# The assignment check of a mixture-of-experts kernel as an all-engine `If`, with list, weights and transposes in another order

## The chip, the cores and the metric

The program runs on one core of one Trainium2 chip. The metric is the device time of one execution, in microseconds. A core has TensorE (PE; its weight loads are shown apart as PEld), VectorE (DVE), ScalarE (ACT), GpSimd (POOL) and SyncE (SP), each with its own instruction queue, and 16 DMA engines that all queues share.

## What is computed

Two parts, one behind the other. A linear attention runs over 4 batches, 8 heads, 768 steps and head width 48. Its output, as 3072 rows ("tokens") of 384 numbers, goes through a balanced mixture of 8 experts: each expert takes exactly 3072 / 8 = 384 tokens. The assignment is greedy over all logits in falling order, and each expert is a two-layer network with 1024 hidden numbers, in float32:

```python
    logits = x @ w_gate
    order = np.argsort(-logits.flatten())
    for idx in order:
        tok, e = (int(idx) // E, int(idx) % E)
        if assigned[tok] >= 0 or counts[e] >= cap:
            continue
        assigned[tok] = e
        counts[e] += 1
    for e in range(E):
        mask = assigned == e
        h = np.maximum(x[mask] @ w1[e], 0.0)
        out[mask] = h @ w2[e]
```

## The kernel before

The program has three stretches. The first, some 205 us, is the attention. It is written twice, `attention_mild` for decays near one and `attention_any` for others, and an `If` on all engines (L975) chooses; with these inputs the mild arm runs. It works through 24 units of 128 tokens, writes their rows to memory (`x_rows`) and their logits to the tile `LG`. The second stretch finds the first expert's tokens. The third, from about 243 us to the end, is the loop over the experts.

**The assignment.** Instead of sorting, `Assignment` fills one expert at a time. A token proposes to the expert of its highest logit; the expert whose 384th proposal has the highest logit is filled first. `likely` (L726) finds that bound by three rounds of `count` (L671). Each round compares every token's maximum `m` with 16 candidates on VectorE (`ind`), sums over tokens on TensorE (`each`, three matmuls of 128 columns of weights), picks and folds on VectorE (`own`, `cnt`, `wide`), spreads the sums on TensorE (`all_ps`), and picks the next candidates on VectorE. The results are `fmax` (which expert), `acc` (which tokens) and `place` (the token's place in the expert's list). If the count of accepted tokens is exactly 384 and the expert is the only one, `flag` (L791) is 1. Otherwise `surely` (L797) does the whole thing exactly, in eight rounds of counts. With these inputs the flag is 1 each time, so `surely` never runs, but its code stands in the program.

`fill` (L695) runs `likely`, loads the flag into a register of TensorE and of VectorE (L703), and chooses between the two bodies of a `Switch` on these two engines (L705): `surely`, or nothing. Then `leave` (L713 to L724) strikes out the expert's column and the accepted tokens in `LG` and brings `taken` and `last` up to date. `remainder` (L869) does the last expert, without a check.

**The list.** `tokens` (L902) turns `place` into `tok`, the numbers of the 384 tokens, as three columns of 128: five VectorE operations up to `vals`, six matmuls (L919), two VectorE operations, one matmul (L929), and two VectorE operations up to `tok` (L936).

**The expert loop.** `fetch` for the expert that comes next does, in this order: `load_weights` (a number on VectorE, a register load on SyncE at L996, and two DMAs of 1.5 MB each on SyncE's queue, L999 and L1001), `tokens`, three indirect DMAs on GpSimd's queue that gather 128 rows of 384 numbers each (L1010), and the transposes: for each of the three blocks of 128 tokens three matmuls against the identity (L1016) and one copy by ScalarE (L1017). `expert` does the network: eight blocks of the hidden layer (`h_ps`, L1025), with a Relu on ScalarE for each (L1026), then three blocks of outputs (`o_ps`, L1030), each copied by ScalarE (L1032) and scattered by an indirect DMA of GpSimd (L1033). A float32 matmul of 128x128x384 is two instructions in the trace, so the hidden layer is 48 and an output block 16.

**What sets the order.** The code of turn n is: `fill` and `fetch` for expert n+1, then `expert` for n. A planner turns it into the queues of the engines: it goes by the order of the code, and where an instruction's inputs are not there yet by its estimate, it puts later ones ahead of it. So hidden matmuls of expert n stand between the counts for expert n+1. The body of a conditional stays together as one piece. Each engine then runs its own queue strictly in that order.

**PSUM.** There are eight banks. Before, the assignment uses three (`each`, `all_ps`, and one that its other results share), the transposes one, the hidden and the output blocks two each. Weights, gathered rows (`xg`) and their transposes (`xT`) have two buffers each, `tok` has three.

Of the kernel before, what the change touches and what calls it, by code (L numbers as in the profile page):

```python
# [10 lines left out]
F32 = mybir.dt.float32  # L11
# [7 lines left out]
PSUM = bass.MemoryType.PSUM  # L19
# [493 lines left out]
class Assignment:  # L513
# [17 lines left out]
    ND = 16  # L531
    G = 8
# [135 lines left out]
    def tt(self, out, a, b, op):  # L668
        self.nc.vector.tensor_tensor(out=out, in0=a, in1=b, op=op)  # L669

    def count(self, pool, m, prop, cand, digit_of):  # L671

        nc, ps, tt = self.nc, self.ps, self.tt
        NT, E, ND, G = self.NT, self.E, self.ND, self.G
        ind = pool.tile([128, NT, ND], BF16, name="ind")
        tt(ind, self.by_token(m, ND), self.by_expert(cand), ALU.is_ge)
        each = ps.tile([128, G, E], F32, name="each")
        for j in range(NT // G):
            nc.tensor.matmul(each.rearrange("p i e -> p (i e)"),  # L679
                             ind[:, ts(j, G), :].rearrange("p i d -> p (i d)"),  # L680
                             prop[:, ts(j, G), :].rearrange("p i e -> p (i e)"),
                             start=(j == 0), stop=(j == NT // G - 1))
        own = pool.tile([128, G, E], F32, name="own")
        tt(own, each, self.same, ALU.mult)
        cnt = pool.tile([128, E], F32, name="cnt")
        nc.vector.tensor_reduce(out=cnt, in_=own.rearrange("p i e -> p e i"), axis=AX.X, op=ALU.add)
        wide = pool.tile([128, ND, E], F16, name="wide")
        tt(wide, digit_of.unsqueeze(2).to_broadcast([128, ND, E]),
           cnt.unsqueeze(1).to_broadcast([128, ND, E]), ALU.mult)
        all_ps = ps.tile([128, ND, E], F32, name="all_ps")  # L690
        nc.tensor.matmul(all_ps.rearrange("p d e -> p (d e)"), self.ones_h,
                         wide.rearrange("p d e -> p (d e)"), start=True, stop=True)
        return all_ps

    def fill(self):  # L695

        nc = self.nc
        out = dict(fmax=self.outs.tile([128, 1], F32, name="fmax"),
                   acc=self.outs.tile([128, self.NT], BF16, name="acc"),
                   place=self.outs.tile([128, self.NT], I32, name="place"))  # L700
        flag = self.likely(**out)
        engines = (mybir.EngineType.PE, mybir.EngineType.DVE)
        sure = nc.values_load(flag[0:1, 0:1], engines=engines, min_val=0, max_val=1,  # L703
                              skip_runtime_bounds_check_because="a truth value")
        for arm in self.tc.Switch({e: sure for e in engines}, 2):  # L705
            if arm == 0:
                with ExitStack() as part:
                    pool = part.enter_context(self.tc.tile_pool(name="surely", bufs=1))
                    self.surely(pool, **out)
        self.leave(out["fmax"], out["acc"])  # L710
        return out["fmax"], out["place"]

    def leave(self, fmax, acc):  # L713

# [154 lines left out]
    def remainder(self):  # L869

        nc, pool = self.nc, self.pool
        sel = pool.tile([128, 2, self.NT], BF16, name="sel")
        nc.vector.memset(sel[:, 1, :], 0.0)
        nc.vector.tensor_scalar(out=sel[:, 0, :], in0=self.taken, scalar1=-1.0, scalar2=1.0,
                                op0=ALU.mult, op1=ALU.add)
        fmax = self.outs.tile([128, 1], F32, name="fmax")
        nc.vector.tensor_scalar(out=fmax, in0=self.last, scalar1=-1.0, scalar2=float(self.E),
                                op0=ALU.mult, op1=ALU.add)
        acc = self.outs.tile([128, self.NT], BF16, name="acc")
        place = self.outs.tile([128, self.NT], I32, name="place")  # L880
        self.places(pool, sel, acc, place)
        return fmax, place

    def places(self, pool, sel, acc, place):

# [55 lines left out]
def rwkv5_eagle_then_base_layer_balanced(  # L941
# [12 lines left out]
    nc = tc.nc  # L954
    N, DX = out.shape
    E, _, F = moe_w1.shape
    NT = N // 128
    CAP = N // E
    NC = CAP // 128
    KD = DX // 128  # L960
    KF = F // 128
# [8 lines left out]
    walk = Assignment(ctx, tc, LG, CAP)  # L970
# [12 lines left out]
    out_rows = dram_disjoint_views(out, NT)  # L983
    wpool = ctx.enter_context(tc.tile_pool(name="weights", bufs=2))
    xpool = ctx.enter_context(tc.tile_pool(name="f_x", bufs=2))
    hpool = ctx.enter_context(tc.tile_pool(name="f_h", bufs=2))
    opool = ctx.enter_context(tc.tile_pool(name="f_o", bufs=3))
    ps_t = ctx.enter_context(tc.tile_pool(name="f_ps_t", bufs=1, space=PSUM))
    ps_h = ctx.enter_context(tc.tile_pool(name="f_ps_h", bufs=2, space=PSUM))
    ps_o = ctx.enter_context(tc.tile_pool(name="f_ps_o", bufs=2, space=PSUM))  # L990

    def load_weights(fmax):
        number = xpool.tile([1, 1], I32, name="number")
        nc.vector.tensor_scalar(out=number, in0=fmax[0:1, :], scalar1=-1.0, scalar2=float(E),
                                op0=ALU.mult, op1=ALU.add)
        e = nc.values_load(number[0:1, 0:1], engines=(mybir.EngineType.SP,), min_val=0, max_val=E - 1,  # L996
                           skip_runtime_bounds_check_because="E less a number from 1 to E")
        w1 = wpool.tile([128, KD, F], F32, name="w1")
        nc.sync.dma_start(w1, moe_w1[ds(e, 1)].rearrange("o (c p) f -> p (o c) f", p=128))  # L999
        w2 = wpool.tile([128, KF, DX], F32, name="w2")  # L1000
        nc.sync.dma_start(w2, moe_w2[ds(e, 1)].rearrange("o (c p) d -> p (o c) d", p=128))  # L1001
        return w1, w2

    def fetch(fmax, place):
        w1, w2 = load_weights(fmax)
        tok = walk.tokens(place)
        xg = xpool.tile([128, NC, DX], F32, name="xg")
        xT = xpool.tile([128, KD, CAP], F32, name="xT")
        for c in range(NC):
            nc.gpsimd.indirect_dma_start(  # L1010
                out=xg[:, c, :], out_offset=None, in_=x_dram,
                in_offset=bass.IndirectOffsetOnAxis(ap=tok[:, c:c + 1], axis=0))
        for c in range(NC):
            xT_ps = ps_t.tile([128, KD, 128], F32, name="xT_ps")
            for f in range(KD):
                nc.tensor.transpose(xT_ps[:, f, :], xg[:, c, ts(f, 128)], ident)  # L1016
            nc.scalar.copy(xT[:, :, ts(c, 128)], xT_ps)  # L1017
        return w1, w2, tok, xT

    def expert(n, w1, w2, tok, xT):  # L1020
        hid = hpool.tile([128, KF, CAP], F32, name="hid")
        for j in range(KF):
            h_ps = ps_h.tile([128, CAP], F32, name="h_ps")
            for f in range(KD):
                nc.tensor.matmul(h_ps, w1[:, f, ts(j, 128)], xT[:, f, :], start=(f == 0), stop=(f == KD - 1))  # L1025
            nc.scalar.activation(hid[:, j, :], h_ps, AF.Relu)  # L1026
        for c in range(NC):
            o_ps = ps_o.tile([128, DX], F32, name="o_ps")
            for j in range(KF):
                nc.tensor.matmul(o_ps, hid[:, j, ts(c, 128)], w2[:, j, :], start=(j == 0), stop=(j == KF - 1))  # L1030
            o_sb = opool.tile([128, DX], F32, name="o_sb")
            nc.scalar.copy(o_sb, o_ps)  # L1032
            nc.gpsimd.indirect_dma_start(  # L1033
                out=out_rows[n * NC + c], out_offset=bass.IndirectOffsetOnAxis(ap=tok[:, c:c + 1], axis=0),
                in_=o_sb, in_offset=None)

    ahead = fetch(*walk.fill())
    for n in range(E):
        here = ahead
        if n + 1 < E:  # L1040
            ahead = fetch(*(walk.fill() if n + 2 < E else walk.remainder()))
        expert(n, *here)


# [26 lines left out]
```

## Time and profile before

| | us |
|---|---|
| median of 3 runs | 593.01 |
| the three runs | 591.62, 593.01, 596.58 |
| the profiled execution | 591.62 |
| its span, first to last instruction | 589.9 |
| busy: PE, DVE, POOL, ACT | 460.3, 217.4, 139.5, 124.3 |
| last attention work of TensorE | 205.5 |
| first hidden matmul | 243.38 |

The mean granted TensorE clock is 0.917 of full speed. The page shows one execution; times in its views count from the first instruction, in microseconds unless marked ns. A row of the timeline names the start, the length, the engine, the source line, the operation with `out<-in` and shapes, and in brackets the idle time of the engine before it with what ended that. A row of a line's view gives least, median and most length in nanoseconds. A "q" behind an engine's name (PEldq) means its sequencer: loads of registers, branches and semaphore waits, which are not counted as busy. Line 1066 is the end of the program, where the pieces of a `Switch` are put in.

The page's slices of the GB/s row show the weights of each expert as a burst (232 to 289 GB/s in the slice in which they come), with little traffic between the bursts.

### The profile page before, as it was taken

To read this page: it belongs to the slowest core of one execution; us is meant where nothing else is said; L and a number is where in the kernel's file an instruction comes from. 1 tells how busy PE (TensorE), PEld (TensorE's weight loads), DVE (VectorE), ACT (ScalarE), POOL (GpSimd) and SP (SyncE) were. 2 spreads that over 40 slices of the span, in tenths; PEclk is the share of its full clock that TensorE was granted. 3 is DMA by queue.
4 is the path that set the end of the run, shared out by engine and by line. 5 is a ranking of instruction groups with operands and counts; after the bars stand their busy time and mean duration, and the time that the engine had idled before them with its cause. 6 is when DMAs were issued, how large, how long until landed. Compare 5 with 4: busy or idle time off the path is not lost. (4 is left out here: it accounts for less than half of the span.)

```text
span 589.9 us, 6607 instructions
## 1 busy us (share of the span) xinstructions
PE 460.3 (78%) x2310; PEld 322.7 (55%) x2310; DVE 217.4 (37%) x664; ACT 124.3 (21%) x255; POOL 139.5 (24%) x178
## 2 busy tenths in 40 slices
PE   0489999999999810569958958959958965999995
PEld 0379888888899700335534524525524533655553
DVE  4787665555572264330251251142142142020000
ACT  0335333333334100112111111111111110121110
POOL 5655555445521002010102101201201201120101
PEclk9999999999999755679979988998998998899999
DMA  6456544444321005260116116107107008250001
GB/s 131 96 110 144 111 102 105 104 98 99 74 54 56 29 4 190 69 232 24 41 24 236 40 14 246 40 4 254 40 5 254 35 10 289 101 160 14 27 1 40
DMA packets 93957, 54.71 MB, mean 93 GB/s; under 512 B 77105, under 2 KB 88498, under 8 KB 93874
## 3 DMA queue, kind: packets, MB, share of 16 engines
q1 hardware_dynamic: 86402, 39.33, 24.3%
q0 software_dynamic: 3072, 9.44, 4.8%
q10 hardware_dynamic: 4400, 4.93, 2.8%
q8 instruction: 40, 0.66, 0.5%
q14 instruction: 43, 0.35, 0.2%
HBM read 44.25 MB, written 9.44 MB: 91 GB/s over the span
## 5 line engine op out<-in xcount | busy, mean ns | idle before, releaser
L1025 PE MATMUL h_ps<-xT,w 128*128 128x384 f32 x384 | 147.7, 534 | 40.3 <-issue 40.3
L1030 PE MATMUL o_ps<-w,hid 128*128 128x384 f32 x384 | 130.3, 493 | 0.0
L1025 PEld LDWEIGHTS h_ps<-xT,w 128*128 128x128 f32 x384 | 74.2, 207 | 88.7 <-issue 58.7
L1030 PEld LDWEIGHTS o_ps<-w,hid 128*128 128x128 f32 x384 | 72.9, 193 | 47.3 <-issue 0.6
L1010 POOL DMA_INDIRECT xg<-x_rows,tok x24 | 23.5, 978 | 204.4 <-PE h_ps L1025 97.2
L1026 ACT ACTIVATE hid<-h_ps 128x384 f32<-128x384 f32 x64 | 31.4, 491 | 152.7 <-PE h_ps L1025 149.3
L1033 POOL DMA_INDIRECT out_dram<-o_sb,tok x24 | 23.6, 985 | 149.4 <-ACT o_sb L1032 124.4
L454 PE MATMUL y_ps<-vt,AT 128*128 128x48 f32 x384 | 46.8, 275 | 2.5 <-DVE AT L437 2.5
L669 DVE TENSOR_TENSOR own<-each,same 128x64 f32<-128x64 f32 x21 | 4.7, 224 | 118.0 <-PE each L679 118.0
L454 PEld LDWEIGHTS y_ps<-vt,AT 128*128 128x128 f32 x384 | 46.1, 195 | 2.9 <-DVE AT L437 2.7
L432 PE MATMUL g_ps<-rB,kT 96*128 96x256 f32 x192 | 45.9, 379 | 0.0
L437 DVE TENSOR_TENSOR AT<-g_ps,mask 128x512 f32<-128x512 f32 x48 | 30.9, 685 | 25.3 <-PE g_ps L432 25.2
L432 PEld LDWEIGHTS g_ps<-rB,kT 96*128 96x128 f32 x192 | 34.6, 191 | 3.6
L397 POOL TENSOR_TENSOR rk<-rt,kt 128x384 f32<-128x384 f32 x24 | 23.9, 998 | 34.9 <-issue 22.5
L1032 ACT COPY o_sb<-o_ps 128x384 f32<-128x384 f32 x24 | 11.5, 479 | 94.7 <-PE o_ps L1030 71.2
L420 ACT ACTIVATE rB<-rT_ps,own 96x512 f32<-96x512 f32 x48 | 30.5, 680 | 3.3 <-PE rT_ps L415 2.6
L1016 PE MATMUL xT_ps<-ident,xg 128*128 128x128 f32 x72 | 14.8, 322 | 20.8 <-DMA xg<-x_rows,tok 15.9
L402 POOL TENSOR_TENSOR yd<-vt,dd 128x384 f32<-128x384 f32 x24 | 20.8, 868 | 36.6 <-DVE xt L458 36.0
L482 ACT COPY xT<-xT_ps 128x384 f32<-128x384 f32 x24 | 11.5, 479 | 80.3 <-PE xT_ps L480 80.3
L1017 ACT COPY xT<-xT_ps 128x384 f32<-128x384 f32 x24 | 11.5, 479 | 76.3 <-PE xT_ps L1016 43.1
L1016 PEld LDWEIGHTS xT_ps<-ident,xg 128*128 128x128 f32 x72 | 8.9, 158 | 33.5 <-DMA xg<-x_rows,tok 20.3
L392 DVE TENSOR_TENSOR ks<-kt,wk 128x384 f32<-128x384 f32 x24 | 24.9, 1048 | 2.6 <-PE kv_ps L465 2.6
(166 smaller groups left out, 490.7 us busy)
## 6 DMA issues: line engine op xcount, KB each, us to landing
w<-in_moe_w_dram SPq DMA_DIRECT2D x16, 1536.0 KB, 7.9
kt<-in_k_dram SPq DMA_DIRECT2D x24, 192.0 KB, 3.1
rt<-in_r_dram SPq DMA_DIRECT2D x24, 192.0 KB, 3.0
vt<-in_v_dram SPq DMA_DIRECT2D x24, 192.0 KB, 2.9
x_rows<-xt ACTq DMA_DIRECT2D x24, 192.0 KB, 2.0
xg<-x_rows,tok POOLq DMA_INDIRECT x24, 3.5
out_dram<-o_sb,tok POOLq DMA_INDIRECT x24, 2.6
u_bc<-in_u_dram ACTq DMA_DIRECT2D x1, 192.0 KB, 4.4
```

The costliest lines, as they stand in the source:

```text
L392: nc.vector.tensor_mul(ks, kt, wk)
L397: nc.gpsimd.tensor_mul(rk, rt, kt)
L420: nc.scalar.activation(rB[:, :, q, :], rT_ps, AF.Copy, scale=own[:, q:q + 1])
L432: nc.tensor.matmul(g_ps[:, 2 * a:2 * a + 2, :].rearrange("p q t -> p (q t)"), kT[:, a, :], rB[:, a].rearrange("p q t -> p (q t)"), start=T ...
L437: nc.vector.tensor_mul(AT[:, hs, :], g_ps[:, hs, :], mask.unsqueeze(1).to_broadcast([128, HP, T]))
L454: nc.tensor.matmul(y_ps[:, ds(h * D, D)], AT[:, h, :], vt[:, ds(h * D, D)], start=first, stop=(h == H - 1), skip_group_check=True)
L1010: nc.gpsimd.indirect_dma_start(out=xg[:, c, :], out_offset=None, in_=x_dram, in_offset=bass.IndirectOffsetOnAxis(ap=tok[:, c:c + 1], axis=0))
L1016: nc.tensor.transpose(xT_ps[:, f, :], xg[:, c, ts(f, 128)], ident)
L1025: nc.tensor.matmul(h_ps, w1[:, f, ts(j, 128)], xT[:, f, :], start=(f == 0), stop=(f == KD - 1))
L1026: nc.scalar.activation(hid[:, j, :], h_ps, AF.Relu)
L1030: nc.tensor.matmul(o_ps, hid[:, j, ts(c, 128)], w2[:, j, :], start=(j == 0), stop=(j == KF - 1))
L1033: nc.gpsimd.indirect_dma_start(out=out_rows[n * NC + c], out_offset=bass.IndirectOffsetOnAxis(ap=tok[:, c:c + 1], axis=0), in_=o_sb, in_of ...
```

## The change

It has five parts.

1. `fill` loads the flag on all engines, and an `If(found < 1)` on all engines takes the place of the `Switch` on two. With the flag at 1 the body, `surely`, is jumped.
2. `tokens` is called in `fill`, ahead of `leave`; the list is made before the expert is struck out.
3. `fetch` issues the gather first and asks for the weights behind it.
4. The transposes leave `fetch`. They become `turn`, called ahead of the last of the three output blocks of the expert at hand; for the first expert ahead of the loop. The network is split into `hidden` and `result` for that.
5. The two results of `count` share one bank (`counts`; columns 0 to 63 and 128 to 255), and the bank that this frees goes to the transposes, which then have two.

The core of the diff:

```diff
@@ count
-        each = ps.tile([128, G, E], F32, name="each")
+        bank = ps.tile([128, 512], F32, name="counts")
+        each = bank[:, 0:G * E].rearrange("p (i e) -> p i e", e=E)
+        all_ps = bank[:, 128:128 + ND * E].rearrange("p (d e) -> p d e", e=E)
...
-        all_ps = ps.tile([128, ND, E], F32, name="all_ps")
@@ fill
-        engines = (mybir.EngineType.PE, mybir.EngineType.DVE)
-        sure = nc.values_load(flag[0:1, 0:1], engines=engines, min_val=0, max_val=1,
-                              skip_runtime_bounds_check_because="a truth value")
-        for arm in self.tc.Switch({e: sure for e in engines}, 2):
-            if arm == 0:
-                with ExitStack() as part:
-                    pool = part.enter_context(self.tc.tile_pool(name="surely", bufs=1))
-                    self.surely(pool, **out)
+        found = nc.values_load(flag[0:1, 0:1], min_val=0, max_val=1,
+                               skip_runtime_bounds_check_because="a truth value")
+        with self.tc.If(found < 1):
+            with ExitStack() as part:
+                pool = part.enter_context(self.tc.tile_pool(name="surely", bufs=1))
+                self.surely(pool, **out)
+        tok = self.tokens(out["place"])
         self.leave(out["fmax"], out["acc"])
-        return out["fmax"], out["place"]
+        return out["fmax"], tok
@@ remainder
-        return fmax, place
+        return fmax, self.tokens(place)
@@ the experts
-    ps_t = ctx.enter_context(tc.tile_pool(name="f_ps_t", bufs=1, space=PSUM))
+    ps_t = ctx.enter_context(tc.tile_pool(name="f_ps_t", bufs=2, space=PSUM))
...
-    def fetch(fmax, place):
-        w1, w2 = load_weights(fmax)
-        tok = walk.tokens(place)
+    def fetch(fmax, tok):
         xg = xpool.tile([128, NC, DX], F32, name="xg")
-        xT = xpool.tile([128, KD, CAP], F32, name="xT")
         for c in range(NC):
             nc.gpsimd.indirect_dma_start(
                 out=xg[:, c, :], out_offset=None, in_=x_dram,
                 in_offset=bass.IndirectOffsetOnAxis(ap=tok[:, c:c + 1], axis=0))
+        return (xg, tok, *load_weights(fmax))
+
+    def turn(xg):
+        xT = xpool.tile([128, KD, CAP], F32, name="xT")
         for c in range(NC):
             xT_ps = ps_t.tile([128, KD, 128], F32, name="xT_ps")
             for f in range(KD):
                 nc.tensor.transpose(xT_ps[:, f, :], xg[:, c, ts(f, 128)], ident)
             nc.scalar.copy(xT[:, :, ts(c, 128)], xT_ps)
-        return w1, w2, tok, xT
+        return xT
...
     ahead = fetch(*walk.fill())
+    xT = turn(ahead[0])
     for n in range(E):
-        here = ahead
+        _, tok, w1, w2 = ahead
         if n + 1 < E:
             ahead = fetch(*(walk.fill() if n + 2 < E else walk.remainder()))
-        expert(n, *here)
+        hid = hidden(w1, xT)
+        for c in range(NC):
+            if c == NC - 1 and n + 1 < E:
+                xT = turn(ahead[0])
+            result(n, c, hid, w2, tok)
```

`hidden` and `result` hold the two loops of `expert` unchanged, `result` for one output block.

More of the change, by code (lines that the diff above doesn't have):

```diff
@@ L1017, in fetch, with hidden @@
             nc.scalar.copy(xT[:, :, ts(c, 128)], xT_ps)
-        return w1, w2, tok, xT
-    def expert(n, w1, w2, tok, xT):
+        return xT
+    def hidden(w1, xT):
         hid = hpool.tile([128, KF, CAP], F32, name="hid")
@@ L1026, in expert, with result @@
             nc.scalar.activation(hid[:, j, :], h_ps, AF.Relu)
[L1027 to L1035, printed above, removed]
+        return hid
+    def result(n, c, hid, w2, tok):
+        o_ps = ps_o.tile([128, DX], F32, name="o_ps")
+        for j in range(KF):
+            nc.tensor.matmul(o_ps, hid[:, j, ts(c, 128)], w2[:, j, :], start=(j == 0), stop=(j == KF - 1))
+        o_sb = opool.tile([128, DX], F32, name="o_sb")
+        nc.scalar.copy(o_sb, o_ps)
+        nc.gpsimd.indirect_dma_start(
+            out=out_rows[n * NC + c], out_offset=bass.IndirectOffsetOnAxis(ap=tok[:, c:c + 1], axis=0),
+            in_=o_sb, in_offset=None)
     ahead = fetch(*walk.fill())
+    xT = turn(ahead[0])
     for n in range(E):
-        here = ahead
+        _, tok, w1, w2 = ahead
         if n + 1 < E:
             ahead = fetch(*(walk.fill() if n + 2 < E else walk.remainder()))
-        expert(n, *here)
+        hid = hidden(w1, xT)
[3 more added lines that the diff above has]
+            result(n, c, hid, w2, tok)
 _INS = ['r', 'k', 'v', 'w', 'u', 'moe_w_gate', 'moe_w1', 'moe_w2']
```

## The prediction

> **What bounds the kernel now.** First the page's busy times (busy us, share of the span, instructions).
>
> ```profile
> PE 460.3 (78%) x2310; PEld 322.7 (55%) x2310; DVE 217.4 (37%) x664; ACT 124.3 (21%) x255; POOL 139.5 (24%) x178
> ```
>
> TensorE is busy for 78% of the span, no other engine for more than 37%. Next the busy time by stretches (columns: stretch, its length, busy time with instructions of PE, PEld, DVE, ACT and POOL, then the granted clock, DMA share, GB/s): one period of the expert loop, and the end, where nothing is left to assign.
>
> ```profile
> 307.10:351.80 44.70, 35.84 (x126) 20.08 (x126) 13.62 (x62) 6.80 (x14) 5.87 (x6) 0.92 0.28 99
> 527.20:583.20 56.00, 55.72 (x177) 32.52 (x177) 0.00 (x0) 9.73 (x20) 5.29 (x6) 1.00 0.07 25
> ```
>
> In the end TensorE has no gap and the full clock. In the loop it idles 44.70 - 35.84 = 8.9 us of each period, at a mean clock of 0.92. The waits (engine and line waiting, what ended it, total us, times, longest) say on what:
>
> ```profile
> PE h_ps L1025 <- issue: 40.3, 6, 7.1
> ...
> PE xT_ps L1016 <- DMA xg<-x_rows,tok: 15.9, 7, 4.8
> ```
>
> "Issue" is time that no semaphore explains. Those six waits stand behind the `Switch` of `fill`, which the code runs seven times. The timeline of one of them (start, length, engine, line, operation):
>
> ```profile
> 390.03 1.54 PE L1025 MATMUL h_ps<-xT,w 128*128 128x384 f32 x4
> 390.13 0.49 ACT L1026 ACTIVATE hid<-h_ps 128x384 f32<-128x384 f32 x1 [1.56 <-PE h_ps L1025]
> ...
> 390.45 0.16 DVE L791 SCALAR_TENSOR_TENSOR flag<-upto,n_sole 128x1 int32<-128x1 f32 x1
> ...
> 398.13 5.11 PE L1025 MATMUL h_ps<-xT,w 128*128 128x384 f32 x8 [6.56 <-issue]
> ```
>
> The flag stands at 390.61, TensorE's work in flight ends at 391.57, and it goes on at 398.13. What its sequencer does meanwhile, by source line (nanoseconds: least/median/most, then first and last start); first the load of the flag, then the branches of this one check:
>
> ```profile
> L703 PEldq TENSOR_LOAD <-flag x7: 306/307/321, 219.0 to 480.4; - x7
> ```
>
> ```profile
> L1066 PEldq COMPARE_BRANCH  x2: 2723/3220/3717, 391.3 to 395.3; - x2
> ```
>
> The load is 0.31 us. The two branches, into the empty arm and out of it, are 3.72 + 2.72 = 6.44 us: they are the stall. The program's only other condition, the choice of the attention arm (L975), is already an `If` on all engines:
>
> ```profile
> L975 SPq COMPARE_BRANCH  x2: 43/46/49, 4.2 to 176.8; - x2
> ...
> L975 PEldq COMPARE_BRANCH  x2: 92/1972/3852, 4.3 to 204.1; - x2
> ```
>
> On TensorE it costs 0.09 us not jumped (at 4.3), and 3.85 where it jumps over the whole other attention arm (at 204.1).
>
> **The sum, against this execution's span of 589.9 us.** The time given for it is 591.62, so 1.7 lies around the span; the median of the runs, 593.01, is 1.4 above that.
>
> *The branch* (six in the loop). The 40.3 us go, and for each check a price S comes. On TensorE: the load ends some 0.35 after the flag, the branch starts near 391.05; a near jump and the semaphore that evens out the skipped arm would end near 391.4, before the array runs dry at 391.57. Low end S = 0. High end, a jump as dear as the far one: 391.05 + 3.85 - 391.57 = 3.3. What is jumped is `surely`: by the code some 70 instructions on TensorE and 100 on VectorE, far less than an attention arm. I take S = 0.5, near the 0.09 row, with something for what the trace does not show. Minus 40.3, plus 3.0.
>
> On VectorE a cheap check is free, since the matmul that needs its list stands eight hidden matmuls behind the check:
>
> ```profile
> 403.07 0.31 PE L919 MATMUL some_ps<-vals,row 128*128 128x48 f16 x6
> ```
>
> ScalarE, GpSimd and SyncE get a load and a branch that they did not have. Behind ScalarE's wait stand the Relus, and behind those TensorE with its two `h_ps` banks; the last Relu ahead of the check began at 390.13, before the flag, and ScalarE idles 1.56 us before a Relu, so a check of under 1.5 us costs nothing there, and each us beyond costs about one. GpSimd has the scatters ahead of its check and the gather behind it:
>
> ```profile
> 380.40 0.98 POOL L1033 DMA_INDIRECT out_dram<-o_sb,tok  x1 [4.17 <-DVE cnt L686]
> ```
>
> The last scatter is gone 9 us before the flag. Behind SyncE's check stand only weights, which have the rest of an expert as cover.
>
> *The clock after the stall.* The eight matmuls behind each of the six stalls, measured as six stretches (the row of their sum), and eight undisturbed ones:
>
> ```profile
> sum 28.40, PE 28.39 PEld 14.46; mean PE 4.73 PEld 2.41
> ```
>
> ```profile
> 405.35 2.74 PE L1030 MATMUL o_ps<-w,hid 128*128 128x384 f32 x8
> ```
>
> 28.40 - 6 x 2.74 = 12.0 us are lost. With a gap of 0.5 I take that as gone: minus 12.0; at S = 3.3 about 1 us a check would stay.
>
> *Transposes at the last third.* The nine transposes and three copies of an expert stay; they move behind two of its three output blocks, so after the check the gather has 14 hidden and 32 output matmuls to land in, at 0.33 us each (11.78 for 36, below) 15.1 us. The list takes about 5 us from the check, the first gather is issued 1 us later, the third 2.6 after that, and a gather lands in 3 to 6 us: the first after 9 to 12, which is when the transposes can start. So the 15.9 us of waits go; with the cover gone they stay at about 2.2 each. They also had a price in clock. The 36 matmuls after the wait of 2.58 us, against 36 after another wait:
>
> ```profile
> 367.02 12.55 PE L1030 MATMUL o_ps<-w,hid 128*128 128x384 f32 x36
> ```
>
> ```profile
> 321.37 11.78 PE L1030 MATMUL o_ps<-w,hid 128*128 128x384 f32 x36
> ```
>
> And the same transposes after the longest wait, 4.80 us, and after one of 1.38 (stretch, length, busy time, clock 0.58 and 1.00):
>
> ```profile
> 501.50:505.60 4.10, 2.01 (x9) 1.46 (x9) 0.58 0.67 259
> 409.40:412.20 2.80, 1.52 (x9) 0.93 (x9) 1.00 0.36 111
> ```
>
> 0.8 + 1.3 = 2.1. Minus 15.9 and minus 2.1. [...]
>
> *Lead-in, before the first hidden matmul.* Here nothing covers the chain.
>
> ```profile
> 218.56 0.16 DVE L791 SCALAR_TENSOR_TENSOR flag<-upto,n_sole 128x1 int32<-128x1 f32 x1
> ...
> 225.30 0.23 DVE L718 TENSOR_SCALAR fe<-first_e,fmax 128x8 f32<-128x8 f32 x1 [6.15 <-issue]
> ...
> 230.12 0.15 DVE L936 TENSOR_REDUCE tok<-mine 128x3 int32<-128x12 f32 x1
> ...
> 231.32 1.14 POOL L1010 DMA_INDIRECT xg<-x_rows,tok  x1 [47.16 <-DVE wide L669]
> ```
>
> ```profile
> 237.90 0.87 PE L1016 MATMUL xT_ps<-ident,xg 128*128 128x128 f32 x3 [4.63 <-DMA w<-in_moe_w_dram]
> ...
> 243.38 3.33 PE L1025 MATMUL h_ps<-xT,w 128*128 128x384 f32 x6
> ```
>
> ```profile
> w<-in_moe_w_dram SPq DMA_DIRECT2D x2, 1536.0 KB, 10.3
> xg<-x_rows,tok POOLq DMA_INDIRECT x3, 6.2
> ```
>
> The check falls from 6.6 us (flag to 225.30) to about 1.4: minus 5.2. The striking out (L718 to L724) no longer stands ahead of the list: about minus 1.0 of the 5.0 from 225.30 to the list. The last row is the gather's time to landing here, beside the weights; over the whole run its median is 3.5. With the weights asked later the overlap starts later: minus 1.3, half the difference. But the weights come later themselves, 10.3 us after an issue near 225, and the first hidden matmul waits for both, so nothing more. Minus 7.5, and the first hidden matmul near 236; 5 to 9 is possible.
>
> *Edits with no price.* The two results of a count in one bank: `own` reads the first before `wide`, and `wide` before the second is written, so they never overlap. A second bank for the transposes saves waits on ScalarE's copy that other matmuls fill already. The striking out behind the list is needed by the next fill's maxima; its 1 us has some 20 us until the counts that use it. The weights, asked some 5 us later in each loop, are used some 20 us after landing.
>
> 589.9 - 40.3 + 3.0 - 12.0 - 15.9 - 2.1 - 7.5 = 515.1; with 1.7 around the span and 1.4 to the median: **518 us**. From the other side: a period's busy time without the lost clock, 35.84 - 2.0, and 0.5 for the check is 34.3; from 236 seven of them, an eighth expert of 96 matmuls (31.4), and the 6.7 after 583.2 end at 514.
>
> **Rivals.** *The jump misses.* For it: each taken branch that the rows show on TensorE costs 2.7 to 3.9 us. Against it: their targets lay in another arm or behind a whole attention arm; and SyncE, whose arm is the shortest, went from its jump at 176.8 to its next branch at 177.3:
>
> ```profile
> L1066 SPq COMPARE_BRANCH  x7: 33/33/38, 177.3 to 443.3; - x7
> ```
>
> Price: 3.3 of stall and 1 of clock in six checks instead of 0.5, +23, and +2.7 in the lead-in: 543. If VectorE alone misses, the list is 2.7 us late, about 2.2 of it uncovered, six times: 531. I put the case at 538. [...]
>
> *The check stays as dear as now.* If an all-engine condition brings two dear branches as the `Switch` does, 40.3, 12.0 and the 5.2 of the lead-in stay, and the 3.0 is not added: 518 + 54.5 = 572. Against it stands the 92 ns.
>
> *The gather is still late.* The cover of 15.1 us against 12 has 3 to spare; if the planner puts the transposes earlier, 7 x 2.2 = 15 come back: 533.
>
> *Slower.* All engines now meet at the check. If that keeps the planner from putting hidden matmuls between the counts of the next fill, TensorE idles through the count chain, as before the lead-in, where only that chain runs, from here to the flag at 218.7, 13.1 us:
>
> ```profile
> 205.62 0.07 DVE L873 MEMSET sel<- 128x12 uint32 x1 [5.02 <-PE lg_ps L485]
> ```
>
> Six of them are 79, and 12 of clock: 609. It decides from (593 - 518) / 6 = 12.5 us a check on. Against it: the `Switch` held TensorE in the same way, and at 390 hidden matmuls stand ahead of it.
>
> **How the numbers follow.** Forecast 0.62, jump misses 0.20, gather late 0.08, check as dear 0.05, slower 0.03, and 0.02 for a run well under the sum. The time is the likeliest case's, 518, by itself 510 to 526. The range goes up to the dear end of the missing jumps, 543, which takes in the late gather, and down to 508, where S = 0 and the lead-in's 9 lead with 5 us for the bounds of the rest; left out are the check as dear, the slower case and the fast one, 1 in 10. About 1% is what a measurement of this kernel can tell from no change: faster by more than that 0.95, within it 0.02, slower 0.03.
>
> **What would show it.** In the profile after: no "issue" group of TensorE of 40 us, and branches of its queue near 0.1 us (2.7 or more: the jump misses); matmuls behind a check at the full clock; no wait of the transposes on the gather; a period of 34 to 35 us in place of 44.7; the first hidden matmul near 236 in place of 243.4. Wrong would make it: TensorE idle through the counts, Relus or scatters late behind a check, or a first hidden matmul that waits for weights.

## The result, and the profile after

| | median, us | runs | ratio to before, 95% interval |
|---|---|---|---|
| before | 594.8 | 591.62 to 597.17 | |
| changed | 516.19 | 512.82 to 520.52 | 0.866 [0.857, 0.876] |

The changed kernel is 13% faster. Ratios and intervals, here and below, leave out runs that were more than 1.5% above the fastest of their kernel, so they are not always the quotient of the medians. Its profiled execution took 512.82, with a span of 511.1 and a mean clock of 0.957 (before: 589.9 and 0.917). The span lost 589.9 - 511.1 = 78.8 us. From the page of the changed kernel: busy times, the clock in 40 slices, and a group (busy, mean ns of one, idle before).

```profile
PE 442.6 (87%) x2310; PEld 315.9 (62%) x2310; DVE 214.6 (42%) x664; ACT 122.8 (24%) x255; POOL 139.4 (27%) x178
...
PEclk9999999999999997556999999999999999999998
...
L1026 PE MATMUL h_ps<-xT,w 128*128 128x384 f32 x384 | 136.0, 502 | 0.9
```

The hidden matmuls (now L1026) had 40.3 us of idle time before them and have 0.9. The four low clock slices (12.8 us each) lie between 192 and 243 us, so the last of them reaches some 8 us into the first hidden layer (first hidden matmul at 234.91); behind them each is at 9 up to the last. Of TensorE's waits on the gather one is left, in the lead-in:

```profile
PE xT_ps L1017 <- DMA xg<-x_rows,tok: 6.2, 1, 6.2
```

The check itself, by the view of one line (ns least/median/most, first and last start). First the branches of the old `Switch` on TensorE over all seven checks:

```profile
L1066 PEldq COMPARE_BRANCH  x14: 2720/3200/4008, 219.7 to 485.0; - x14
```

Then the changed kernel's:

```profile
L705 PEldq COMPARE_BRANCH  x7: 202/218/341, 217.3 to 418.1; - x7
...
L705 DVEq COMPARE_BRANCH  x7: 56/56/63, 217.8 to 418.3; - x7
L705 DVEq EVENT_SEMAPHORE  x7: 21/21/21, 218.4 to 418.9; - x7
```

Seven jumps of 0.2 to 0.34 us on TensorE stand where fourteen branches of 2.7 to 4.0 stood. Below is TensorE's timeline, with one row of its weight loads (PEld), from the last sums ahead of a check to the next period, whose counts begin at 304.00; the counts before began at 269.74.

```profile
280.33 0.17 PE L780 MATMUL st_ps<-acc,rest_of 128*128 128x24 bf16 x1
280.36 3.86 PE L1026 MATMUL h_ps<-xT,w 128*128 128x384 f32 x10
...
282.01 1.59 PEld L1026 LDWEIGHTS h_ps<-xT,w 128*128 128x128 f32 x6 [0.73 <-issue]
...
284.59 0.32 PE L919 MATMUL some_ps<-vals,row 128*128 128x48 f16 x6 [0.37 <-DVE vals L669]
...
287.53 10.48 PE L1033 MATMUL o_ps<-w,hid 128*128 128x384 f32 x32
297.85 0.82 PE L1017 MATMUL xT_ps<-ident,xg 128*128 128x128 f32 x6
...
304.00 0.25 PE L681 MATMUL counts<-prop,ind 128*128 128x64 bf16 x3
```

The ten hidden matmuls span the check, and no gap between them is long enough for a row of its own. The check still holds TensorE up a little: its weight loads stand idle for 0.73 us before 282.01. The only gap that the trace puts down to another engine is 0.37 us, for the list; such a wait stands at four of the six checks of the loop. The transposes find their rows there. The period is 304.00 - 269.74 = 34.3 us, before 44.3 to 46.4.

The lead-in, in the timeline of all engines:

```profile
216.42 0.16 DVE L791 SCALAR_TENSOR_TENSOR flag<-upto,n_sole 128x1 int32<-128x1 f32 x1
...
218.46 0.18 DVE L907 TENSOR_SCALAR lo<-place 128x24 int32<-128x24 int32 x1 [1.45 <-DVEq L705]
...
221.12 0.13 DVE L994 TENSOR_SCALAR number<-fmax 1x1 int32<-1x1 f32 x1
...
222.24 0.41 SPq L999 DMA_DIRECT2D w<-in_moe_w_dram  x1
...
222.81 0.16 DVE L936 TENSOR_REDUCE tok<-mine 128x3 int32<-128x12 f32 x1
...
224.03 1.14 POOL L1007 DMA_INDIRECT xg<-x_rows,tok  x1 [41.06 <-DVE cnt L688]
...
230.84 0.87 PE L1017 MATMUL xT_ps<-ident,xg 128*128 128x128 f32 x3 [6.17 <-DMA xg<-x_rows,tok]
...
234.91 0.99 PE L1026 MATMUL h_ps<-xT,w 128*128 128x384 f32 x1
```

From the flag to the first hidden matmul it is 234.91 - 216.58 = 18.3 us, before 243.38 - 218.72 = 24.7. One thing in it is not as the code reads: the weights (222.24) are still asked for ahead of the gather (224.03). Their number needs only `fmax`, and the planner put it into a gap of VectorE ahead of `tok`.

### The profile page after: what moved, and what is told of

It reads as the page before. It is cut to its first block, busy times and chain, and to the rows that moved or that the text cites. A ratio compares the mean times of both kernels' runs of the same rounds, so it can differ in the third digit from the quotient of the medians.

```text
span 511.1 us, 6583 instructions
## 1 busy us (share of the span) xinstructions
PE 442.6 (87%) x2310; PEld 315.9 (62%) x2310; DVE 214.6 (42%) x664; ACT 122.8 (24%) x255; POOL 139.4 (27%) x178
## 5 line engine op out<-in xcount | busy, mean ns | idle before, releaser
L1026 PE MATMUL h_ps<-xT,w 128*128 128x384 f32 x384 | 136.0, 502 | 0.9
L1033 PE MATMUL o_ps<-w,hid 128*128 128x384 f32 x384 | 127.5, 486 | 0.0
L1026 PEld LDWEIGHTS h_ps<-xT,w 128*128 128x128 f32 x384 | 69.1, 192 | 45.0 <-issue 10.2
L1007 POOL DMA_INDIRECT xg<-x_rows,tok x24 | 23.4, 975 | 148.0 <-PE h_ps L1026 63.6
L1036 POOL DMA_INDIRECT out_dram<-o_sb,tok x24 | 23.6, 985 | 128.3 <-ACT o_sb L1035 123.1
L454 PE MATMUL y_ps<-vt,AT 128*128 128x48 f32 x384 | 46.4, 274 | 1.9 <-DVE AT L437 1.9
L669 DVE TENSOR_TENSOR own<-counts,same 128x64 f32<-128x64 f32 x21 | 4.7, 225 | 102.0 <-PE counts L681 102.0
L432 PEld LDWEIGHTS g_ps<-rB,kT 96*128 96x128 f32 x192 | 34.6, 191 | 3.6
L482 ACT COPY xT<-xT_ps 128x384 f32<-128x384 f32 x24 | 11.5, 478 | 79.8 <-PE xT_ps L480 79.8
L458 DVE TENSOR_TENSOR xt<-y_ps,yd 128x384 f32<-128x384 f32 x24 | 13.4, 557 | 30.7 <-PE y_ps L454 29.3
L412 PE MATMUL kT_ps<-ident,ks 128*96 128x128 f32 x96 | 16.1, 289 | 11.2 <-DVE ks L392 11.1
L398 POOL TENSOR_TENSOR rk<-rk,u_bc 128x384 f32<-128x384 f32 x24 | 24.8, 1034 | 1.7
```

Source lines behind the costliest of these rows:

```text
L398: nc.gpsimd.tensor_mul(rk, rk, u_bc)
L432: nc.tensor.matmul(g_ps[:, 2 * a:2 * a + 2, :].rearrange("p q t -> p (q t)"), kT[:, a, :], rB[:, a].rearrange("p q t -> p (q t)"), start=T ...
L454: nc.tensor.matmul(y_ps[:, ds(h * D, D)], AT[:, h, :], vt[:, ds(h * D, D)], start=first, stop=(h == H - 1), skip_group_check=True)
L1007: nc.gpsimd.indirect_dma_start(out=xg[:, c, :], out_offset=None, in_=x_dram, in_offset=bass.IndirectOffsetOnAxis(ap=tok[:, c:c + 1], axis=0))
L1036: nc.gpsimd.indirect_dma_start(out=out_rows[n * NC + c], out_offset=bass.IndirectOffsetOnAxis(ap=tok[:, c:c + 1], axis=0), in_=o_sb, in_of ...
```

## The experiments

The medians below are of four runs (six for the three arms in a row, the one bank for the transposes, the unchanged kernel and the late weight load), beside a kernel before of 594.13, 591.75 and 594.75 us in the three groups.

**The condition alone, and the transposes alone.** First, the kernel before with only the new condition:

```diff
-        for arm in self.tc.Switch({e: sure for e in engines}, 2):
+        with self.tc.If(found < 1):
```

> The kernel before with the all-engine If alone; transposes, list, weights and banks as before. Theory A, the terms add: the stall (39.4 us), its slow clock (12.0) and some 5 us of the lead-in go, the waits of the transposes on the gather stay near 16 us: about 593 - 57 = 536. Theory B, the stall was also cover for the list: without it only 22 matmuls (about 8 us with the work in flight) stand between the flag and the transposes, while list and gather take 10 to 13 us, so the waits grow from 16 to 25-35 us: about 546 to 556.

Measured: 560.73 (557.14 to 564.8), ratio 0.947 [0.941, 0.954]. The gain is 33 us, not the 40.3 of stall and 12.0 of clock. TensorE's wait and one gather, in the views of this kernel:

```profile
PE xT_ps L1014 <- DMA xg<-x_rows,tok: 25.3, 8, 4.5
```

```profile
337.64 2.74 PE L1028 MATMUL o_ps<-w,hid 128*128 128x384 f32 x8
344.34 0.55 PE L1014 MATMUL xT_ps<-ident,xg 128*128 128x128 f32 x3 [3.95 <-DMA xg<-x_rows,tok]
344.73 1.18 PE L1028 MATMUL o_ps<-w,hid 128*128 128x384 f32 x2
```

The waits for the gather grew from 15.9 to 25.3 us, and slow matmuls stand behind them (two in 1.18 us; 0.81 where nothing waits, as a row below shows). By the page TensorE's busy time is 458.4 us here, 460.3 before and 442.6 in the changed kernel, so hardly any of the slow clock's price has gone. So the stall had been partly a cover: in the kernel before, at the check at 390, VectorE went on at 396.69 and TensorE at 398.13, so the list had a start of 1.4 us that is gone when TensorE does not stop. The mechanism is the one of theory B, and its waits are in the range; the time, 560.73, is above its 546 to 556.

Then the kernel before with only the transposes moved:

```diff
-        return w1, w2, tok, xT
+        return xg, tok, w1, w2
...
+            if c == NC - 1 and n + 1 < E:
+                xT = turn(ahead[0])
```

> The kernel before with the transposes ahead of the last output block and nothing else (Switch, list, weights and banks as before). Both theories: the 15.9 us of waits on the gather and about 2 us of slow clock go, the stall at the check stays near 40 us: about 575. If B holds, this edit is worth more beside the If than here: the sum of e1's and this gain falls short of the whole gain by 10 to 20 us; if A holds, they add up to it within 4 us.

Measured: 578.12 (572.85 to 581.1), ratio 0.972 [0.963, 0.980], as expected. The two gains alone are 33.4 + 16.0 = 49.4 us; the whole change brings 78.6. Some 29 us belong to neither part alone, but to their being together (and 4 of them to the second bank for the transposes, below). That is more than the 10 to 20 us that theory B gave it.

**The Switch put back into the changed kernel.** The edit of the first experiment backwards.

> The changed kernel with the Switch on TensorE and VectorE back. The stall of 40 us, 12 us of slow clock and 5 us of the lead-in come back: 516 + 56 = about 572, with two branches of 3.7 and 2.7 us per check on TensorE's queue. A rival, that the new order of list, weights and transposes gives TensorE other work to do during the check: under 550.

Measured: 571.78 (566.02 to 577.14), ratio 0.961 [0.953, 0.968]. In the changed kernel the condition is worth 571.78 - 516.19 = 56 us, in the old one 33: only where the transposes come behind two output blocks does its whole gain stay.

**The order put back.** The list again behind the striking out, the weights again ahead of the list and the gather:

```diff
-        tok = self.tokens(out["place"])
         self.leave(out["fmax"], out["acc"])
...
+        w1, w2 = load_weights(fmax)
+        tok = walk.tokens(place)
```

> The changed kernel with the list made behind the striking out and the weights asked for ahead of the gather. My theory: both are covered in the loop, and only the lead-in feels them: plus 0 to 3 us, so within 1% of the changed kernel (514 to 522). A rival, that the order counts for each expert: about 1 us each or more, plus 7 to 15 us, and waits of the transposes on the gather or of the hidden matmuls on weights.

Measured: 517.54 (516.35 to 519.1), ratio 0.872 [0.867, 0.877]: no difference to the changed kernel. Two of the change's five parts do nothing that can be measured.

**What the price of the jump goes by.** The arm that is jumped (by the code some 70 instructions on TensorE and 100 on VectorE) stands eight times in a row; it is never run:

```diff
+            for _ in range(8):
                 with ExitStack() as part:
```

> The changed kernel with the exact assignment written eight times in the arm that is jumped over (never run with these inputs): the jump gets eight times as long, some 590 instructions on TensorE and 800 on VectorE, and nothing that runs is changed. Theory, the price of a check is the fetch of its target: branches of 2.7 to 3.9 us on TensorE's queue, VectorE 2 us later, 2.5 to 3.5 us of stall per check and about 1 us of slow clock, 2.7 in the lead-in: 516 + 20 to 30 = 536 to 546. Rival, a taken compare-and-branch has a fixed price whatever its distance: branches stay near 0.25 us and the time at 516.

Measured: 549.41 (544.92 to 552.29), ratio 0.924 [0.916, 0.933]. The branch's line, with who waited for it (us, times):

```profile
L705 PEldq COMPARE_BRANCH  x7: 3304/3602/3762, 224.1 to 451.3; - x7
L705 DVEq COMPARE_BRANCH  x7: 56/56/69, 224.6 to 451.5; - x7
...
  DVE lo L908: 23.6, 7
  PE h_ps L1027: 19.8, 6
```

The same condition costs TensorE 3.6 us over eight arms, where it costs 0.22 over one (medians of the branch), so here an `If` on all engines is cheap only over the short arm. (The kind of condition counts too: over the same short arm the `Switch` above stalls TensorE for 39.2 us in the loop.) The theory's 2.7 to 3.9 us for the branch came. That the branch waits for the fetch of its target was not shown; the page of this kernel counts more instruction packets than the changed kernel's (queue, packets, MB; the changed kernel has 22 and 27):

```profile
q8 instruction: 33, 0.54, 0.4%
q14 instruction: 36, 0.29, 0.2%
```

A size between the two, three arms in a row:

> The arm that is jumped over stands three times in a row (222 instructions on TensorE, about 300 on VectorE). If the price of the jump goes by its length, TensorE's branch takes about 1.5 us, the same in all checks, and the whole is about 524 us. If it goes by whether the landing place has been brought in already, the branch shows two kinds of values, 0.2 to 0.35 us or 2 to 4 us and nothing between; the whole then lies between 516 (all near) and 545 us (all far).

Measured: 540.36 (539.61 to 548.08), ratio 0.914 [0.907, 0.921]. The line of the branch, and the timeline at one check:

```profile
L705 PEldq COMPARE_BRANCH  x7: 219/328/406, 219.6 to 442.2; - x7
...
L705 DVEq COMPARE_BRANCH  x7: 56/63/63, 220.1 to 442.4; - x7
L705 DVEq EVENT_SEMAPHORE  x7: 21/21/21, 223.2 to 445.4; - x7
...
  DVE lo L908: 23.4, 7
```

```profile
287.71 3.86 PE L1027 MATMUL h_ps<-xT,w 128*128 128x384 f32 x10
...
291.83 0.18 DVE L908 TENSOR_SCALAR lo<-place 128x24 int32<-128x24 int32 x1 [3.07 <-DVEq L705]
...
294.23 0.46 DVE L669 TENSOR_TENSOR oh<-hi,hi_of 128x288 f16<-128x288 int32 x1 [1.14 <-issue]
...
295.38 0.42 PE L920 MATMUL some_ps<-vals,row 128*128 128x48 f16 x6 [3.81 <-DVE vals L669]
```

Neither expectation as it stood: both spoke of TensorE alone. TensorE jumps its 210 instructions in 0.33 us; VectorE, with some 300, starts its next instruction 3.1 us after its branch (223.2 against 220.1). Over all seven checks VectorE waits 23.4 us behind its branch, as long as with eight arms (23.6); in the changed kernel it is 6.0. So on VectorE the price rose from some 100 to 300 instructions, and from 300 to some 800 no further, and each engine has its own. On TensorE 70 and 210 instructions cost 0.2 to 0.4 us and some 560 cost 3.6. And VectorE's stall reaches TensorE nearly whole: ten hidden matmuls stand between the check and the matmuls of the list, which cover the check of the changed kernel but for 0.37 us. At the check shown, 3.1 us at the branch and 1.1 behind it are 3.8 us of idle time on TensorE; at the five others of the loop it idles 2.7 to 2.9. Against the unchanged kernel of the same group (517.17) the whole is 23 us.

**The Switch with its empty body first.** In the changed kernel, with a `Switch` on the opposite of the flag, so that the empty body is the nearer one:

```diff
+        for arm in self.tc.Switch({e: unsure for e in engines}, 2):
+            if arm == 1:
```

> The changed kernel with the Switch back, but with the empty body first and the exact assignment second (one more small VectorE operation turns the flag around). If the Switch's price is where its bodies lie: the entry now goes to the body next to the branch and costs under 1 us on TensorE, only the exit over the other body costs 2.7; per check 3 us in place of 6.4, about 516 + 25 = 541. If the indirect branch is dear whatever its target: entry 3.7 and exit 2.7 as before, about 572.

Measured: 564.29 (562.26 to 565.95), ratio 0.950 [0.943, 0.957], between the two expectations and nearer the dear one. The line of its branches on TensorE, over all checks and then in the stretch of one:

```profile
L1078 PEldq COMPARE_BRANCH  x14: 296/4060/4912, 221.5 to 464.9; - x14
...
L1078 PEldq COMPARE_BRANCH  x2: 296/2492/4687, 299.5 to 300.1; - x2
```

From the second check on the way in is near (0.30 to 0.38 us), and the way out, over the exact body, became dearer, 4.6 to 4.9 us instead of 2.7; only at the first check is the way in far too (3.5 us). The old kernel paid for two far jumps, this one for one, but a dearer one: TensorE's stall in the loop falls only from 39.2 us (with the `Switch` put back as it was) to 32.9. Why the way out became dearer is not shown. Turning the bodies round saves 7.5 us of the 31 that the first theory gave it.

**No check at all.** The load of the flag, the condition and the exact assignment behind it are left out.

> The changed kernel without the check: the flag is not loaded, there is no branch and the exact assignment is left out; the rest runs as it does. It shows what the check still costs. Theory, the check is nearly free on TensorE: about 1 us in the loop and 1.5 us in the lead-in, so 512 to 516. Rival, the check still costs TensorE or ScalarE 1 us or more each time in a place that the waits do not show: 508 or less.

Measured: 508.39 (506.72 to 511.45), ratio 0.858 [0.851, 0.865]; 7.8 us less than the changed kernel. The same stretch of TensorE's timeline as above:

```profile
277.66 0.17 PE L774 MATMUL st_ps<-acc,rest_of 128*128 128x24 bf16 x1
277.68 4.76 PE L1020 MATMUL h_ps<-xT,w 128*128 128x384 f32 x14
282.28 0.31 PE L913 MATMUL some_ps<-vals,row 128*128 128x48 f16 x6
...
283.93 10.48 PE L1027 MATMUL o_ps<-w,hid 128*128 128x384 f32 x32
```

From the sums to the first output matmul it is 283.93 - 277.66 = 6.27 us, with the check 287.53 - 280.33 = 7.20, so the check costs 0.93 us there. Of these, 0.37 is the wait for the list. Most of the rest falls where TensorE itself loads the flag, jumps and waits for the semaphore: ten hidden matmuls at the check last 3.86 us, and here fourteen last 4.76, which less four of 0.33 leaves 3.45, so by difference some 0.4 us goes there. Whole periods differ by 0.84 (34.26 and 33.42), and by 3.9 in all over the five periods from 269.74 on. In the lead-in and the first period, which the planner filled in another order, the check costs 3.5 us more from the flag to the counts at 269.74 (53.2 us, here 49.6). The spans behind the flag differ by 7.1, the medians by 7.8. So the check costs more than the theory's 2.5 us, and the rival's 1 us or more each time is nearer; its 508 is missed by 0.4.

**The banks.** Both edits of PSUM taken back (`each` and `all_ps` in banks of their own, one bank for the transposes), and then only the second of them:

```diff
-    ps_t = ctx.enter_context(tc.tile_pool(name="f_ps_t", bufs=2, space=PSUM))
+    ps_t = ctx.enter_context(tc.tile_pool(name="f_ps_t", bufs=1, space=PSUM))
```

> The changed kernel with the two results of a count in banks of their own and one bank for the transposes. Theory: the second bank for the transposes saves only waits on ScalarE's copies, which output matmuls fill: within 1% of the changed kernel (514 to 520). Rival: with one bank the transposes wait for two copies of 0.48 us per expert with nothing to fill in: plus 7 x 1 to 2 us, 523 to 530.

> The changed kernel with one bank for the transposes instead of two, the counts bank still shared. By the stretches of the kernel with both edits of the banks taken back, one bank costs 0.38 us in each of 7 last thirds (16.94 against 16.55 us), 2.7 us, and about 1 us in the lead-in: 3 to 4 us over the unchanged kernel of this job, about 520. Rival (the second transposes bank explains all of the 9 us by which that kernel was slower): 525 or more.

Measured: 525.61 (520.1 to 526.77), ratio 0.882 [0.874, 0.890], with both taken back; 521.55 (517.03 to 525.25), ratio 0.881 [0.873, 0.888], with one bank for the transposes, against 517.17 for the unchanged kernel of its group. The lead-in and the last third with one bank, on TensorE's timeline:

```profile
235.23 0.88 PE L1017 MATMUL xT_ps<-ident,xg 128*128 128x128 f32 x3 [6.16 <-DMA xg<-x_rows,tok]
...
240.70 1.65 PE L1026 MATMUL h_ps<-xT,w 128*128 128x384 f32 x2 [0.52 <-ACT xT L1018]
```

```profile
294.20 10.48 PE L1033 MATMUL o_ps<-w,hid 128*128 128x384 f32 x32
304.52 0.49 PE L1017 MATMUL xT_ps<-ident,xg 128*128 128x128 f32 x3
304.84 0.81 PE L1033 MATMUL o_ps<-w,hid 128*128 128x384 f32 x2
305.67 0.55 PE L1017 MATMUL xT_ps<-ident,xg 128*128 128x128 f32 x3
...
311.05 0.25 PE L681 MATMUL counts<-prop,ind 128*128 128x64 bf16 x3
```

Each group of transposes waits until ScalarE has emptied the bank. In the lead-in that is 240.70 - 235.23 = 5.5 us from the first transposes to the first hidden matmul instead of 4.1. In the loop the two output matmuls put in between are not long enough: from the first output matmul to the next counts it is 311.05 - 294.20 = 16.85 us instead of 304.00 - 287.53 = 16.47. Together 1.4 + 7 x 0.38 = 4.1 us, the 3 to 4 us that were expected. The medians differ by 4.4, with runs that spread over 5 and 8 us; the size is the trace's, and the times agree. The kernel with both edits back misses its theory (514 to 520) and lands in the rival's range, but not by the rival's 1 to 2 us an expert. The rest of its 9 us is not in its loop, whose periods are those of one transposes bank (34.64 us in both). Its profiled execution lost time in the attention: its flag stands at 224.99 us, with one transposes bank at 220.98 and in the changed kernel at 216.58. Against the one bank for the transposes another 0.9 us lies between the flag and the counts of the next period. For its other three runs there is no profile. By the windows (length, PE busy, clock, DMA share, GB/s):

```profile
20.00:40.00 20.00, 13.04 (x65) 0.89 0.40 79
40.00:60.00 20.00, 19.98 (x133) 0.85 0.54 119
```

The changed kernel's profiled execution, in the same windows:

```profile
20.00:40.00 20.00, 13.44 (x89) 1.00 0.45 88
40.00:60.00 20.00, 19.98 (x162) 1.00 0.68 150
```

**The weights really behind the gather, and the yardstick.** The changed kernel unchanged, and with the first expert's second weight load made to wait for the gathered rows:

```diff
+            nc.gpsimd.tensor_single_scalar(out=zero, in_=behind, scalar=0.0, op=ALU.mult)
...
+            nc.gpsimd.tensor_tensor(out=later, in0=number, in1=zero, op=ALU.add)
```

> The changed kernel once more, unchanged, as the yardstick of this job. Both theories: about 516 us (513 to 521). The profiles so far show the clock at about 0.86 between 20 and 60 us of the attention stage in some executions and at 1.00 in others, whatever the edit, worth about 5 us; if that is chance, single times of this kernel fall into two groups some 5 to 7 us apart.

> Only the first expert's second weight load waits until its gather has landed. Theory (the 3 MB asked for ahead of the gather share its way): the wait of the first transposes for the gather falls from 6.2 us to between 3.5 and 5, the time from the first flag to the first hidden matmul from 18.3 us to about 16.5 to 17.5, the whole by 1 to 2 us, so within 1% of the unchanged kernel of this job. Rival (the first load alone is in the way): the wait stays at about 6 and nothing is gained.

Measured: 517.17 (516.11 to 521.4), ratio 0.877 [0.870, 0.883], for the unchanged kernel, and 515.67 (513.86 to 520.04), ratio 0.873 [0.866, 0.879], with the late load. The six runs of the unchanged kernel stand in two groups, four from 516.1 to 517.9 and two at 520.7 and 521.4, some 4 us apart, near the 5 to 7 of the expectation; only one of the first group has a profile. The gather's wait in the kernel with the late load:

```profile
PE xT_ps L1024 <- DMA xg<-x_rows,tok: 5.3, 1, 5.3
```

The wait fell only from 6.1 to 5.3 us, between the theory's 3.5 to 5 and the rival's 6; that the first load, still ahead of the gather, holds the rest is likely and not shown. By the matmuls' starts the first period took 35.5 us instead of 34.6. What the lead-in won (0.7 us) the first period gave back, and 1.5 us of median lie inside the spread. No kernel with the check is measurably faster than the changed one in these runs.

## Why the prediction was right

Forecast 518, measured 516.19. The rivals: the `Switch`'s price staying (572) is what the Switch put back measures, 571.78; a late gather and a TensorE idle through the counts did not come. Step by step, with spans:

- *The branch, -40.3 + 3.0.* The 40.3 went to 0.9. S was taken as 0.5 and is about 0.8 (3.9 us over five periods), so some 4.6 for six, as an estimate. The guess is near TensorE's own part (some 0.4 to 0.6 where it was worked out), but not by its reasons: it let TensorE's branch start near 391.05, 0.44 us after the flag, while the row beside it has the old branches start at 391.3, and the new one starts 0.7 us after its flag (217.3 and 216.58). "On VectorE a cheap check is free" left VectorE's part out: it is 0.37 us at four of the six checks. The matmuls in front of the list cover a cheap check and nothing beyond. With that, the rival's "2.2 of it uncovered" and 531 for VectorE alone were too low: with three arms 2.7 to 3.8 us were uncovered, and the time was 540.
- *The jump misses* (0.20) was the right rival to fear. Its price (543) is near what eight arms show, 549, and the reason against it, the short arm, is what decided.
- *The clock, -12.0, and the gather's, -15.9 and -2.1.* They came whole: in the loop there is no wait for the gather, the clock slices are at 9, and the busy time of hidden and output matmuls fell from 147.7 and 130.3 us to 136.0 and 127.5, by 14.5 where 12.0 + 2.1 were forecast. The prediction took the two gains one after the other; the first experiment shows that the first is only worth 33 alone. The sum was right because both were in it.
- *Lead-in, -7.5.* It was -6.3. The check went from 6.6 to 1.9 us (predicted 1.4), and the list from 5.0 to 4.5 (218.46 to 222.97; predicted 4.0). The gather's -1.3 did not come (its wait is 6.2 us here): the weights are still asked for ahead of it; "the overlap starts later" took the order of the code for the order of the queues. In its place came 1.4 us from the second bank for the transposes.
- *Edits with no price.* The second transposes bank was said to save "waits that other matmuls fill already". It saves 4.1 us: two output matmuls (0.65 us) do not fill a round of transposes and copy (1.15 us with one bank, 304.52 to 305.67 above). The shared counts bank is worth nothing in the loop, and the order of list, striking out and weights nothing that the times show, as said.
- That the total is so near is in part luck. S too small by some 1.6 and a lead-in 1.2 short of its gain stand against the 2.7 that the second transposes bank saves in the loop and that the sum left out. The span came out 4.0 us below the sum. Of these, 2.1 are an attention that ended earlier: the flag, ahead of which nothing was changed but the counts' bank, stands at 216.58 instead of 218.72, and the executions above differ by more than that there. The rest, some 2 us, was not traced to a step.

## What to carry to other kernels

A stall on the bounding engine may be the cover of a transfer or of another engine's chain: ask what runs in its shadow before its whole length is booked as gain, and price the edits that need each other together. Here a jump over rare code cost under 1 us a check with some 70 instructions of it on TensorE and 100 on VectorE, and with three times as many the whole took 23 us more, so keep such an arm short and look at each engine's count of instructions. Where a short matmul group, a copy and the next group take turns, compare a round of group and copy with the matmuls that stand in between: here those were shorter (0.65 us against 1.15), and a second PSUM bank paid (4.1 us in all).

## What the runs showed that was not expected

- A dear jump looks different on the two engines. TensorE's shows as a long branch (3.3 to 3.8 us over eight arms); VectorE's branch takes 63 ns over three arms and its next instruction starts 3.1 us after it, so the branch's own row hides the price.
- With one, three and eight arms the jump became dear between some 100 and 300 instructions on VectorE, and between some 210 and 560 on TensorE. The instruction packets rise too: the page counts 22 on the first queue with one arm, 26 with three and 33 with eight, and on the second 27, 36 and 36. With three arms only VectorE's jump was dear, and only the second queue stands at its count of eight arms; no row of the page says which queue serves which engine.
- The attention between 20 and 60 us ran at a clock of 0.85 to 0.89 (windows of 20 us) in three of the fourteen profiled executions, in a fourth, with the `Switch` put back, two slices of the page stand at 7 and 8 tenths, and in the ten others it ran at 1.00, whatever the edit. In both rows above for 40 to 60 us TensorE is busy for 19.98 of 20 us, with 133 matmuls against 162. The copy of the attention's last logits began at 210.4 to 212.6 us in the four and at 203.9 to 208.0 in the ten. What sets it was not found. It makes a difference of 1% between two kernels of this family hard to read from four runs.
